# Sigmoid attention with a bilinear feed-forward on one core: float32 scores by row halves in nine pairs, weight decoding in two steps, last product turned round

## The chip, the cores and the metric

The kernel runs on one core of one Trainium2 chip. The metric is the device time of one execution in microseconds, lower is better.

## The reference

```python
S = 448; scale = 1/sqrt(64)                      # 8 batches, 12 heads, 448 tokens, head size 64
scores = scale * (q @ k^T) - log(S)
attn   = sigmoid(scores)
x      = (attn @ v)                              # -> 3584 tokens x 768
a = x @ w1; b = x @ w2                           # w1, w2: 768 x 1024
out = ((a * b) @ w3) @ w_out                     # w3: 1024 x 1024, w_out: 1024 x 768
```

q, k and v are float32; the four weights arrive as 8-byte floats, which the kernel decodes itself, from two 32-bit words to one float32.

## The kernel before

**Precision.** A product of two float32 operands is made in one of two ways. *Split*: each operand is cut into a high and a low part of type fp32r (a copy that rounds, and a subtraction), and three products hi·hi, hi·lo, lo·hi are added in PSUM. *Plain*: one float32 matmul, which the profile records as two matmul records of two passes each.

**Attention.** The 48 head pairs (8 batches of 6) are walked in order, each in 4 slots, one for each chunk of 128 keys (the last of 64). A slot numbers 4·p + i. In a slot TensorE makes the scores of one chunk (`scores`, L184, into the PSUM tile `sp`, two buffers), ScalarE the sigmoid (L169), and one slot later TensorE the product with v (`attend`, L233 or L240, into `av`). In the first `PLAIN` = 12 pairs scores are four fp32r matmuls (the head's q is stacked as high over low rows, so that K is 128) and the product with v is plain, in column halves of the array: the two heads write PSUM rows 0 to 63 and 64 to 127 (L233). In the other pairs all is split: `split_pair` makes qs, kh, kl and ks (VectorE, and GpSimd for kl and ks), the last chunk of both heads is done by `short_scores` (L210), and the product with v takes four fp32r matmuls a chunk (L240).

**Filler.** From slot 26 on each slot also holds 12 matmuls of x @ w1 and x @ w2 of the batch before (`up`, L300, 448 columns), so that batch b's filler runs in batch b+1; the last batch's runs after the attention.

**Weights.** `decode_weights` is a generator with 16 jobs for w1 and w2 (768 KB each) and 24 for w3. One step of it loads the raw words up to three jobs ahead (`load_words`, tile `raw`, three buffers), takes the magnitude on ScalarE (L76), decodes in six VectorE instructions (L83 to L99) and splits the result (a cast L66 on ScalarE, a subtraction L67 on VectorE).

**Order.** Engines named in `manual_schedule` issue in the order of the program text: TensorE and SyncE (SP) throughout the attention, ScalarE and GpSimd too in the first two pairs. The other engines' order is chosen when the kernel is built. All loads and stores are issued by SP, which waits in order for the buffer that the next transfer writes. The tile tag `qk` has three buffers and a pair takes two of them (q and k, each loaded twice, to partitions 0 to 63 and 64 to 127).

**End.** After the attention: w_out is decoded beside the last filler, w3 @ w_out is made (L442, 384 columns), and the last product (L460) takes 128 tokens at a time as the stationary operand and 384 columns of w3·w_out as the moving one.

Of the kernel before, what the change touches and what calls it, by code (L numbers as in the profile page):

```python
# [25 lines left out]
def sigmoid_attention_bilinear_ffn(  # L26
# [6 lines left out]
    w2: bass.AP,  # L33
    w3T: bass.AP,
    w_out: bass.AP,
    out: bass.AP,
):


# [1 line left out]


    nc = tc.nc
    B, D, H, S = qT.shape
    DM, DF = w1.shape[0], w1.shape[1] // 2
    NT = B * S
    P = 128
# [17 lines left out]
    def split(dst_hi, dst_lo, src, hi_engine, lo_engine):  # L65
        hi_engine(out=dst_hi, in_=src)  # L66
        lo_engine.tensor_tensor(out=dst_lo, in0=src, in1=dst_hi, op=ALU.subtract)  # L67

    def load_words(src, pool=pd):
        raw = pool.tile([P, *src.shape[1:-1], 2], U32, name="raw")  # L70
        nc.sync.dma_start(out=raw, in_=src)
        return raw

    def magnitude(raw):
        f = pd.tile([P, *raw.shape[1:-1]], F32, name="f")
        nc.scalar.activation(f, raw[..., 1].bitcast(F32), AF.Abs, scale=HW_SCALE)  # L76
        return f
# [40 lines left out]
    nc.scalar.activation(ready, bias, AF.Sigmoid)  # L118

    def load_pair(b, hp):  # L120
        qq = pa.tile([P, 2, S], F32, name="qq", tag="qk", bufs=3)
        kk = pa.tile([P, 2, S], F32, name="kk", tag="qk", bufs=3)
        for dst, src in ((qq, qT), (kk, kT)):
            for r in range(2):
                nc.sync.dma_start(out=dst[r * D:(r + 1) * D], in_=src[b, :, 2 * hp:2 * hp + 2])  # L125
        return qq, kk

    def load_v(b, hp):
# [7 lines left out]
            nc.sync.dma_start(out=vv[r * D:(r + 1) * D, NC - 1], in_=v[b, full:, cols])  # L136
        return vv

    def split_pair(plain, first, qq, kk):

        qs = pa.tile([P, 2, S], F32R, name="qs")
        kh = pa.tile([P, 2, S], F32R, name="kh")
        kl = pa.tile([P, 2, S], F32R, name="kl")
        copy = nc.scalar.copy if plain else nc.vector.tensor_copy
        (nc.vector.tensor_copy if first else copy)(out=qs, in_=qq)
        nc.vector.tensor_tensor(out=qs[D:], in0=qq[D:], in1=qs[D:], op=ALU.subtract)  # L146
        split(kh, kl, kk, copy, nc.vector if plain else nc.gpsimd)
        if plain:
            return qs, kh, kl, None
# [111 lines left out]
    def words(w, columns):  # L261
        return w.rearrange("(c p) (f u) -> p c f u", p=P, u=2)[:, :, columns]

    def decode_weights():

        step = NK // 2
        jobs = [
            (n, fc, slice(0, NK), words(w, slice(fc * P, (fc + 1) * P)))
            for fc in range(NF) for n, w in ((1, w1), (2, w2))
        ]  # L270
        n_up = len(jobs)
        jobs += [
            (3, ic, slice(at, min(at + step, NF)), words(w3T, slice(ic * P, (ic + 1) * P)))
            for ic in range(NF) for at in range(0, NF, step)
        ]
        raws, fs = [], []
        for i, (n, at, cs, _) in enumerate(jobs):
            end = n_up if i < n_up else len(jobs)
            while len(raws) < min(i + (3 if i < n_up else 2), end):
                _, _, ks, src = jobs[len(raws)]  # L280
                raws.append(load_words(src[:, ks], pp if len(raws) < n_up else pd))
            while len(fs) < min(i + 2, end):
                fs.append(magnitude(raws[len(fs)]))
            f = decode(raws[i], fs[i])
            if n == 3:
                nc.sync.dma_start(out=w3_dram[at, :, cs], in_=f)
            else:
# [27 lines left out]
    def take(stream, n):  # L315
        for _ in range(n):
            next(stream, None)
# [6 lines left out]
    qks = {p: load_pair(*pairs[p]) for p in range(2)}  # L324
    vvs = {0: load_v(*pairs[0])}
    splits, vs = {0: split_pair(0 < PLAIN, True, *qks.pop(0))}, {}
    weights = decode_weights()
    xs = {b: [] for b in range(B)}
    filler = iter(())
# [18 lines left out]

    chunks = [0, NC - 1, *range(1, NC - 1)]
    ups = -(-(NF * 2 * NK * 3) // (NPAIR * NC))  # L350

    pieces = {1, 7, 13, 19} | {NPAIR * NC + i for i in range(3 * NF) if i % 3 < 2}
    slot = 0
    for p, (b, hp) in enumerate(pairs):
        if p == 2:
            order.close()
            order.enter_context(tc.manual_schedule(engines={ET.PE, ET.SP}))
        plain = p < PLAIN
        if p == PLAIN - 1:
            take(weights, 2 * NF - len(pieces & set(range(slot))))  # L360
            phase_p.close()
            pf.append(phase_a.enter_context(tc.tile_pool(name="pf", bufs=2, side="right")))
        if p + 2 < len(pairs):
            qks[p + 2] = load_pair(*pairs[p + 2])
        if p + 1 < len(pairs):
            vvs[p + 1] = load_v(*pairs[p + 1])
        vs[p] = split_v(plain, vvs.pop(p))
        qs, kh, kl, ks = splits.pop(p)
        for i, c in enumerate(chunks):
            if not plain and i == 1:  # L370
                short = short_scores(ks, qs)
            else:
# [4 lines left out]
            if i == min(p, 1) and p + 1 < len(pairs):  # L377
                splits[p + 1] = split_pair(p + 1 < PLAIN, p == 0, *qks.pop(p + 1))
# [30 lines left out]
    for jc in range(NF):  # L409
        take(filler, 10)  # L410
        for half in range(2):
            ms = slice(half * NM, (half + 1) * NM)
            src = w_out[jc * P:(jc + 1) * P].rearrange("p (m u) -> p m u", u=2)[:, ms]
            raw = load_words(src)
# [10 lines left out]
    def load_g(tb):  # L425
        g = p4.tile([P, NF, P], F32, name="graw")
        nc.sync.dma_start(out=g, in_=g_dram[:, :, tb * P:(tb + 1) * P].rearrange("f p t -> p f t"))
        gh = p4.tile([P, NF, P], F32R, name="gh")
        gl = p4.tile([P, NF, P], F32R, name="gl")
        split(gh, gl, g, nc.scalar.copy, nc.vector)  # L430
        return gh, gl

    for ic in range(NF):
        w3h, w3l = w3s.pop(ic)
        if ic + 1 < NF:
# [10 lines left out]
            split(w34h[:, ic, ms], w34l[:, ic, ms], acc[:, :NM], nc.scalar.copy, nc.vector)  # L446


    gs = {0: load_g(0)}
    for tb in range(NT // P):  # L450
        if tb + 1 < NT // P:
            gs[tb + 1] = load_g(tb + 1)
        gh, gl = gs.pop(tb)
        o_sb = p4.tile([P, DM], F32, name="o_sb", bufs=3)
        for half in range(2):
            ms = slice(half * NM, (half + 1) * NM)
            acc = ps.tile([P, 512], F32, name="up", tag=next(banks), bufs=2)
            for fc in range(NF):
                for m, (a, w) in enumerate(((gh, w34h), (gh, w34l), (gl, w34h))):
                    nc.tensor.matmul(  # L460
                        acc[:, :NM], a[:, fc], w[:, fc, ms],
                        start=(fc == 0 and m == 0), stop=(fc == NF - 1 and m == 2),
                    )
            nc.vector.tensor_copy(out=o_sb[:, ms], in_=acc[:, :NM])  # L464
            nc.sync.dma_start(out=out[tb * P:(tb + 1) * P, ms], in_=o_sb[:, ms])
    phase_w.close()


# [24 lines left out]
```

## Time and profile before

| | |
|---|---|
| median of 3 runs | 1102.95 us (1102.86 to 1105.55) |
| profiled execution | 1105.32 us, its span 1103.5 us |
| TensorE busy | 1075.5 us (97%), 5424 records |
| VectorE, ScalarE, GpSimd busy | 729.2 (66%), 566.2 (51%), 203.7 us (18%) |
| HBM | read 102.37 MB, written 29.88 MB, 120 GB/s |

The span is the time from the first to the last instruction; 1.8 us of the profiled execution lie outside it. Matmul ends are modelled and matmuls overlap, so that the time of one is read from start to start. "SPq" rows are SP's issues of transfers.

### The profile page before, as it was taken

What the parts mean: (1) busy time and instruction counts of PE and PEld (TensorE: products, weight loads), DVE (VectorE), ACT (ScalarE), POOL (GpSimd) and SP (SyncE); (2) the same over time, 40 slices, a digit from 0 to 9 for tenths busy, and PEclk for the clock granted to TensorE, in tenths of its full rate; (3) what the DMA queues carried; (4) which work ended last, traced back from release to release, by engine and by line L of the source; (5) the groups of instructions that cost most, each with busy time, mean ns of one, the idle gap of its engine ahead of it and who ended that gap; (6) DMA issues with size and microseconds to landing.
All of it is one profiled execution on the core that took longest, in us unless ns stands there. A gap on an engine that the chain in (4) does not pass through costs nothing.

```text
span 1103.5 us, 14939 instructions
## 1 busy us (share of the span) xinstructions
PE 1075.5 (97%) x5424; PEld 961.9 (87%) x5424; DVE 729.2 (66%) x1119; ACT 566.2 (51%) x792; POOL 203.7 (18%) x256
## 2 busy tenths in 40 slices
PE   3899999999999999999999999999999999999998
PEld 1347678899999989999999899999999999999998
DVE  4678997897988879888788987758732122222222
ACT  3786645677677677767677676753322011111110
POOL 0000012343433433234333333300000000000000
PEclk8999999999999999999999999999999999999999
DMA  8488837354344543545345443115341133333331
GB/s 219 124 198 238 216 102 189 99 141 122 104 122 105 150 103 101 145 105 141 96 116 159 116 120 85 53 44 184 106 123 39 41 102 114 119 101 111 124 100 50
DMA packets 115784, 133.23 MB, mean 121 GB/s; under 512 B 8960, under 2 KB 100352, under 8 KB 115712
## 3 DMA queue, kind: packets, MB, share of 16 engines
q1 hardware_dynamic: 115712, 132.29, 43.2%
q8 instruction: 43, 0.70, 0.3%
q14 instruction: 29, 0.24, 0.1%
HBM read 102.37 MB, written 29.88 MB: 120 GB/s over the span
## 4 chain that ended last, share of the span: by engine, by line
PE 87%; DVE 5%; DMA 4%; issue 1%; SPq 1%; POOL 1%; ACT 1%; DVEq 0%; ACTq 0%; POOLq 0%
PE up L300 38%; PE up L460 21%; PE sp L184 10%; PE av L240 8%; PE up L442 6%; PE av L233 3%; DMA vv<-vL 2%; PE sp L210 1%; DVE al L202 1%; POOL kl L67 1%; SPq L125 1%; DMA raw<-w 1%; DVE qs L146 0%; DMA g_dram<-g 0%; DMA kk<-kT 0%
## 5 line engine op out<-in xcount | busy, mean ns | idle before, releaser
L300 PE MATMUL up<-xh,w 128*128 128x448 f32 x1536 | 466.4, 367 | 0.0
L300 PEld LDWEIGHTS up<-xh,w 128*128 128x128 f32 x1536 | 288.4, 188 | 26.1
L300 PE MATMUL up<-xl,w 128*128 128x448 f32 x768 | 281.3, 366 | 0.0
L460 PE MATMUL up<-w,gh 128*128 128x384 f32 x896 | 227.3, 334 | 0.0
L460 PEld LDWEIGHTS up<-w,gh 128*128 128x128 f32 x896 | 162.0, 188 | 0.0
L67 POOL TENSOR_TENSOR kl<-kk,kh 128x896 fp32r<-128x896 f32 x36 | 102.1, 2836 | 298.2 <-DVE kh L66 234.7
L169 ACT ACTIVATE ah<-sp,bias 128x896 fp32r<-128x896 f32 x108 | 108.7, 1006 | 92.9 <-PE sp L184 92.8
L300 PEld LDWEIGHTS up<-xl,w 128*128 128x128 f32 x768 | 144.2, 188 | 13.1
L460 PE MATMUL up<-w,gl 128*128 128x384 f32 x448 | 149.6, 334 | 0.0
L202 DVE TENSOR_TENSOR al<-sp,ah 128x896 fp32r<-128x896 f32 x108 | 117.7, 1090 | 32.8 <-ACT sp L169 31.0
L464 DVE COPY o_sb<-up 128x384 f32<-128x384 f32 x56 | 31.2, 558 | 160.1 <-PE up L460 160.1
L184 PE MATMUL sp<-qs,kh 128*128 128x448 f32 (+1 forms) x312 | 120.4, 386 | 8.0 <-ACT kh L66 8.0
L66 ACT CAST gh<-graw 128x1024 fp32r<-128x1024 f32 x28 | 29.5, 1053 | 191.8 <-PE up L460 189.3
L184 PE MATMUL sp<-qs,kl 128*128 128x448 f32 (+1 forms) x312 | 115.9, 371 | 0.4 <-DVE kl L67 0.4
L169 ACT ACTIVATE sp<-sp,bias 128x896 f32<-128x896 f32 x108 | 105.0, 973 | 0.0
L184 PEld LDWEIGHTS sp<-qs,kh 128*128 128x128 f32 (+1 forms) x312 | 58.1, 186 | 48.1 <-issue 34.9
L67 POOL TENSOR_TENSOR vs<-vv,vs 128x256 fp32r<-128x256 f32 x72 | 59.3, 838 | 211.0 <-DVE vs L66 172.4
L240 PE MATMUL av<-ah,vs 128*128 128x448 f32 x288 | 94.2, 368 | 1.1 <-DVE t L176 1.1
L460 PEld LDWEIGHTS up<-w,gl 128*128 128x128 f32 x448 | 84.1, 188 | 0.0
L240 PE MATMUL av<-al,vs 128*128 128x448 f32 x216 | 79.3, 367 | 0.6 <-DVE al L202 0.6
L224 DVE TENSOR_TENSOR ah<-st,ah 64x448 fp32r<-64x448 f32 x72 | 49.7, 690 | 26.1 <-ACT st L169 24.5
L184 PEld LDWEIGHTS sp<-qs,kl 128*128 128x128 f32 (+1 forms) x312 | 58.2, 187 | 6.2 <-DVE kl L67 0.8
(57 smaller groups left out, 1351.5 us busy)
## 6 DMA issues: line engine op xcount, KB each, us to landing
qq<-qT SPq DMA_DIRECT2D x96, 224.0 KB, 3.8
kk<-kT SPq DMA_DIRECT2D x96, 224.0 KB, 4.0
g_dram<-g SPq DMA_DIRECT2D x64, 224.0 KB, 1.9
graw<-g_dram SPq DMA_DIRECT2D x28, 512.0 KB, 3.6
raw<-w SPq DMA_DIRECT2D x16, 768.0 KB, 6.2
out<-o_sb SPq DMA_DIRECT2D x56, 192.0 KB, 1.9
vv<-vL SPq DMA_DIRECT2D x48, 192.0 KB, 3.9
raw<-w3T SPq DMA_DIRECT2D x16, 384.0 KB, 4.0
```

Of the source, the lines that this page charges most:

```text
L66: hi_engine(out=dst_hi, in_=src)
L67: lo_engine.tensor_tensor(out=dst_lo, in0=src, in1=dst_hi, op=ALU.subtract)
L169: nc.scalar.activation(dst, src, AF.Sigmoid, bias=bias[:n], scale=scale)
L184: nc.tensor.matmul(sp[:, j], k[:, j, at:at + n], qs[:, j], start=m == 0, stop=m == 1)
L202: nc.vector.tensor_tensor(out=al, in0=sp, in1=ah, op=ALU.subtract)
L224: nc.vector.tensor_tensor(out=a[others, j], in0=t[rows], in1=a[rows, j], op=ALU.subtract)
L233: nc.tensor.matmul(accs[0][cols, :S], v[:ops[0].shape[0], c, cols], ops[0][:, j], start=first, stop=last,)
L240: nc.tensor.matmul(accs[j][:, :S], v[:, c, j].rearrange("p u d -> p (u d)"), a[:, j], start=first and m == 0, stop=last and m == len(ops) - 1,
L300: nc.tensor.matmul(acc[:, :S], w[:, fc, kc], x, start=(kc == 0 and m == 0), stop=(kc == NK - 1 and m == 2),)
L442: nc.tensor.matmul(acc[:, :NM], a[:, jc], w[:, jc, ms], start=(jc == 0 and m == 0), stop=(jc == NF - 1 and m == 2),)
L460: nc.tensor.matmul(acc[:, :NM], a[:, fc], w[:, fc, ms], start=(fc == 0 and m == 0), stop=(fc == NF - 1 and m == 2),)
L464: nc.vector.tensor_copy(out=o_sb[:, ms], in_=acc[:, :NM])
```

## The change

The first nine pairs (`PLAIN` = 9) take their scores straight from q and k: q and k are loaded once, both heads under each other, and each head's scores are one float32 matmul on 64 rows of the array (head 0 on rows 0 to 63, head 1 on rows 64 to 127). Nothing is split in these pairs, and a pair takes one buffer of `qk` instead of two. Pairs 9 to 11 become split pairs. A decoding job is taken in two steps, decode and split, at slots from a list; the raw words have three buffers for the first 12 jobs and one for the others, and are loaded two jobs ahead, then one. ScalarE and GpSimd keep the order of the text until pair 8. The jobs of w3 are 16 instead of 24. The last product has 128 columns of w3·w_out as the stationary operand and 512 tokens as the moving one, and the output is written transposed (the host turns it). q and k lie in memory as batch, head, d, token.

```diff
-    PLAIN = 2 * NPAIR
+    PLAIN = 9
...
-    def load_words(src, pool=pd):
-        raw = pool.tile([P, *src.shape[1:-1], 2], U32, name="raw")
+    def load_words(src, pool=None):
+        if pool is None:
+            raw = pd.tile([P, NK, P, 2], U32, name="raw", bufs=1)[:, :src.shape[1]]
+        else:
+            raw = pool.tile([P, *src.shape[1:-1], 2], U32, name="raw")
...
     def load_pair(b, hp):
+        heads = slice(2 * hp, 2 * hp + 2)
+        if b * NPAIR + hp < PLAIN:
+            qk = pa.tile([P, 2, S], F32, name="qp", tag="qk", bufs=3)
+            for i, src in enumerate((qT, kT)):
+                nc.sync.dma_start(out=qk[:, i], in_=src[b, heads].rearrange("h d s -> (h d) s"))
+            return qk[:, 0], qk[:, 1]
...
+    def split_pair(plain, qq, kk):
+        if plain:
+            return qq, kk, None, None
...
         for j in range(2):
+            if kl is None:
+                rows = slice(j * D, (j + 1) * D)
+                nc.tensor.matmul(sp[:, j], kh[rows, at:at + n], qs[rows], start=True, stop=True)
+                continue
...
+    def load_job(i):
+        _, _, cs, src = jobs[i]
+        raws[i] = load_words(src[:, cs], pp) if i < EARLY else load_words(src[:, cs])
+
     def decode_weights():
         for i, (n, at, cs, _) in enumerate(jobs):
-            end = n_up if i < n_up else len(jobs)
-            while len(raws) < min(i + (3 if i < n_up else 2), end):
-                _, _, ks, src = jobs[len(raws)]
-                raws.append(load_words(src[:, ks], pp if len(raws) < n_up else pd))
-            while len(fs) < min(i + 2, end):
-                fs.append(magnitude(raws[len(fs)]))
-            f = decode(raws[i], fs[i])
+            if i + 2 < EARLY:
+                load_job(i + 2)
+            for k in (i, i + 1):
+                if k not in fs and k in raws:
+                    fs[k] = magnitude(raws[k])
+            f = decode(raws.pop(i), fs.pop(i))
+            if i + 1 >= EARLY and i + 1 < len(jobs):
+                load_job(i + 1)
             if n == 3:
                 nc.sync.dma_start(out=w3_dram[at, :, cs], in_=f)
+                yield
+                continue
+            yield
+            split(wh[n][:, at, cs], wl[n][:, at, cs], f, nc.scalar.copy, nc.vector)
             yield
...
+    first = NPAIR * NC
+    starts = [1 + i * first // 7 for i in range(7)] + [first + 1 + 3 * i // 2 for i in range(8)] + [first + 14]
+    later = [(2 * NPAIR + 2 * i) * NC + 1 for i in range(2 * NF)]
+    steps = starts + [s + 2 - s // first for s in starts] + later
+    EARLY = sum(s < (PLAIN - 1) * NC for s in starts)
+    for p in range(2):
+        qks[p] = load_pair(*pairs[p])
+        load_job(p)
+        if p == 0:
+            vvs[0] = load_v(*pairs[0])
...
-        if p == 2:
+        if p == PLAIN - 1:
             order.close()
             order.enter_context(tc.manual_schedule(engines={ET.PE, ET.SP}))
...
-            if slot in pieces or b > 1 and hp % 3 < 2 and i == 1:
-                take(weights, 1)
+            take(weights, steps.count(slot))
...
+    split_g(0, 1, load_g(0, 1))
+    last = NT // TB - 1
+    for tb in range(NT // TB):
+        for mc in range(DM // P):
+            ms = slice(mc * P, (mc + 1) * P)
             acc = ps.tile([P, 512], F32, name="up", tag=next(banks), bufs=2)
             for fc in range(NF):
+                at = (2 * tb + fc // NH) % 3
+                for m, (w, g) in enumerate(((w34h, ghs), (w34h, gls), (w34l, ghs))):
                     nc.tensor.matmul(
+                        acc[:, :TB], w[:, fc, ms], g[:, at, fc % NH],
                         start=(fc == 0 and m == 0), stop=(fc == NF - 1 and m == 2),
                     )
...
+            nc.vector.tensor_copy(out=o_sb, in_=acc[:, :TB])
+            nc.sync.dma_start(out=outT[ms, tb * TB:(tb + 1) * TB], in_=o_sb)
```

## Rows read from the trace of the kernel before

**Rows 1.** The page's 40 slices of the span: tenths of busy time, tenths of clock.
```profile
PE   3899999999999999999999999999999999999998
PEclk8999999999999999999999999999999999999999
```
**Rows 2.** Stretches: us, busy time (records) of each engine, granted clock, DMA share, GB/s.
```profile
0.00:27.70 27.70, 8.80 (x24) 4.23 (x24) 12.59 (x18) 8.72 (x11) 0.20 (x4) 0.89 0.84 218
27.70:76.70 49.00, 44.87 (x181) 18.82 (x181) 36.24 (x47) 39.37 (x48) 0.00 (x0) 0.96 0.68 166
76.70:172.70 96.00, 96.00 (x443) 67.64 (x441) 83.03 (x121) 54.08 (x68) 3.93 (x6) 1.00 0.68 189
172.70:736.30 563.60, 561.85 (x2743) 513.47 (x2742) 464.14 (x716) 398.30 (x574) 199.54 (x247) 1.00 0.43 114
867.30:1103.50 236.20, 232.93 (x1344) 232.61 (x1342) 63.67 (x83) 27.87 (x27) 0.00 (x0) 1.00 0.31 101
```
**Rows 3.** Timeline of the first 30 us: start, duration, engine, line, operation, [idle before, releaser].
```profile
5.21 0.63 DVE L145 CAST qs<-qq 128x896 fp32r<-128x896 f32 x1 [4.34 <-DMA qq<-qT]
7.05 0.94 ACT L66 CAST kh<-kk 128x896 fp32r<-128x896 f32 x1 [4.83 <-DMA kk<-kT]
8.04 0.74 PE L184 MATMUL sp<-qs,kh 128*128 128x448 f32 x1 [8.04 <-ACT kh L66]
...
13.12 3.29 SPq L71 DMA_DIRECT2D raw<-w  x3
...
19.68 0.89 ACT L76 ACTIVATE f<-raw 128x768 f32<-128x768 f32 x1 [6.25 <-DMA raw<-w]
...
25.93 0.83 ACT L66 CAST w<-f 128x768 fp32r<-128x768 f32 x1 [3.08 <-DVE f L99]
...
27.72 1.76 PE L233 MATMUL av<-ap,vv 128*64 128x448 f32 x4 [10.38 <-ACT ap L169]
```
**Rows 4.** Timeline of TensorE in one slot of batch 0.
```profile
63.03 0.97 PE L233 MATMUL av<-ap,vv 128*64 128x448 f32 x4
63.93 0.47 PE L184 MATMUL sp<-qs,kh 128*128 128x448 f32 x1
...
64.95 0.97 PE L233 MATMUL av<-ap,vv 128*64 128x448 f32 x4
```
**Rows 5.** Timeline of TensorE: where slots 26, 49 and 53 begin.
```profile
76.67 0.47 PE L184 MATMUL sp<-qs,kh 128*128 128x448 f32 x1
...
177.03 0.68 PE L210 MATMUL sp<-qs,ks 128*128 128x448 f32 x2
...
192.66 0.57 PE L210 MATMUL sp<-qs,ks 128*128 128x448 f32 x2
```
**Rows 6.** Timeline of SP and ScalarE from 36 to 48 us: one job's raw words.
```profile
36.55 1.11 SPq L125 DMA_DIRECT2D kk<-kT  x2
...
38.87 0.59 SPq L71 DMA_DIRECT2D raw<-w  x1
...
47.16 0.89 ACT L76 ACTIVATE f<-raw 128x768 f32<-128x768 f32 x1 [2.27 <-DMA raw<-w]
```
**Rows 7.** Timeline of SP from 335 to 348 us: two issues that follow each other.
```profile
335.68 0.53 SPq L286 DMA_DIRECT2D w_dram<-f  x1
347.78 0.32 SPq L312 DMA_DIRECT2D g_dram<-g  x1
```
**Rows 8.** First and last instruction of one decoding on VectorE; GpSimd's group for kl.
```profile
87.69 0.56 DVE L83 TENSOR_SCALAR raw<-raw 128x768 uint32<-128x768 uint32 x1 [1.23 <-ACT f L76]
...
92.43 0.95 DVE L99 TENSOR_TENSOR f<-f,raw 128x768 f32<-128x768 f32 x1
...
L67 POOL TENSOR_TENSOR kl<-kk,kh 128x896 fp32r<-128x896 f32 x36 | 102.1, 2836 | 298.2 <-DVE kh L66 234.7 <-issue 61.3 <-PE sp L184 2.3
```
**Rows 9.** Chain of work: start, us, longest uninterrupted runs of matmuls of 448 and 384 columns.
```profile
736.26 64.43 PE up L300 x312
...
867.27 232.98 PE up L460 x1344
```

More of the change, by code (lines that the diff above doesn't have):

```diff
@@ L35, in sigmoid_attention_bilinear_ffn @@
     w_out: bass.AP,
[L36 removed]
+    outT: bass.AP,
 ):
     nc = tc.nc
[L44 removed]
+    B, H, D, S = qT.shape
     DM, DF = w1.shape[0], w1.shape[1] // 2
@@ L137, in load_v @@
         return vv
[L139 to L145, printed above, removed]
+    def split_pair(plain, qq, kk):
+        if plain:
+            return qq, kk, None, None
+        qs = pf[0].tile([P, 2, S], F32R, name="qs")
+        kh = pf[0].tile([P, 2, S], F32R, name="kh")
+        kl = pf[0].tile([P, 2, S], F32R, name="kl")
+        nc.vector.tensor_copy(out=qs, in_=qq)
         nc.vector.tensor_tensor(out=qs[D:], in0=qq[D:], in1=qs[D:], op=ALU.subtract)
-        split(kh, kl, kk, copy, nc.vector if plain else nc.gpsimd)
-        if plain:
-            return qs, kh, kl, None
+        split(kh, kl, kk, nc.vector.tensor_copy, nc.gpsimd)
         ks = pf[0].tile([P, 2, P], F32R, name="ks")
@@ L323, in sigmoid_attention_bilinear_ffn @@
     pairs = [(b, hp) for b in range(B) for hp in range(NPAIR)]
-    qks = {p: load_pair(*pairs[p]) for p in range(2)}
-    vvs = {0: load_v(*pairs[0])}
-    splits, vs = {0: split_pair(0 < PLAIN, True, *qks.pop(0))}, {}
+    first = NPAIR * NC
+    starts = [1 + i * first // 7 for i in range(7)] + [first + 1 + 3 * i // 2 for i in range(8)] + [first + 14]
+    assert len(starts) == 2 * NF
+    later = [(2 * NPAIR + 2 * i) * NC + 1 for i in range(2 * NF)]
+    steps = starts + [s + 2 - s // first for s in starts] + later
+    EARLY = sum(s < (PLAIN - 1) * NC for s in starts)
+    qks, vvs = {}, {}
+    for p in range(2):
[3 more added lines that the diff above has]
+            vvs[0] = load_v(*pairs[0])
+    splits, vs = {0: split_pair(0 < PLAIN, *qks.pop(0))}, {}
     weights = decode_weights()
@@ L376, in sigmoid_attention_bilinear_ffn @@
                 waiting.append((slot + 1, p, c, attention(plain, sp)))
-            if i == min(p, 1) and p + 1 < len(pairs):
-                splits[p + 1] = split_pair(p + 1 < PLAIN, p == 0, *qks.pop(p + 1))
-            if slot in pieces or b > 1 and hp % 3 < 2 and i == 1:
-                take(weights, 1)
+            if i == 1 and p + 1 < len(pairs):
+                splits[p + 1] = split_pair(p + 1 < PLAIN, *qks.pop(p + 1))
+            take(weights, steps.count(slot))
             if b > 0 and (hp, i) == (0, 2):
@@ L423, in sigmoid_attention_bilinear_ffn, with load_g, split_g @@
     p4 = ctx.enter_context(tc.tile_pool(name="p4", bufs=2, side="left"))
[L425 to L431, printed above, removed]
+    TB = 512
+    NH = NF // 2
+    ghs = pw.tile([P, 3, NH, TB], F32R, name="w")
+    gls = pw.tile([P, 3, NH, TB], F32R, name="w")
+    def load_g(tb, half):
+        g = p4.tile([P, NH, TB], F32, name="graw")
+        fs = slice(half * NH, (half + 1) * NH)
+        nc.sync.dma_start(
+            out=g, in_=g_dram[fs, :, tb * TB:(tb + 1) * TB].rearrange("f p t -> p f t")
+        )
+        return g
+    def split_g(tb, half, g):
+        at = (2 * tb + half) % 3
+        for fs in (slice(0, NH // 2), slice(NH // 2, NH)):
+            split(ghs[:, at, fs], gls[:, at, fs], g[:, fs], nc.scalar.copy, nc.vector)
+    assert NT % TB == 0
+    split_g(0, 0, load_g(0, 0))
     for ic in range(NF):
@@ L446, in sigmoid_attention_bilinear_ffn @@
             split(w34h[:, ic, ms], w34l[:, ic, ms], acc[:, :NM], nc.scalar.copy, nc.vector)
[L449 to L456, printed above, removed]
+    split_g(0, 1, load_g(0, 1))
[3 more added lines that the diff above has]
+            ms = slice(mc * P, (mc + 1) * P)
             acc = ps.tile([P, 512], F32, name="up", tag=next(banks), bufs=2)
             for fc in range(NF):
-                for m, (a, w) in enumerate(((gh, w34h), (gh, w34l), (gl, w34h))):
+                at = (2 * tb + fc // NH) % 3
+                for m, (w, g) in enumerate(((w34h, ghs), (w34h, gls), (w34l, ghs))):
                     nc.tensor.matmul(
-                        acc[:, :NM], a[:, fc], w[:, fc, ms],
+                        acc[:, :TB], w[:, fc, ms], g[:, at, fc % NH],
                         start=(fc == 0 and m == 0), stop=(fc == NF - 1 and m == 2),
                     )
-            nc.vector.tensor_copy(out=o_sb[:, ms], in_=acc[:, :NM])
-            nc.sync.dma_start(out=out[tb * P:(tb + 1) * P, ms], in_=o_sb[:, ms])
+                if (mc, fc) == (DM // P - 1, NH - 1) and tb < last:
+                    split_g(tb + 1, 1, g1)
+            if mc == 0 and tb < last:
+                split_g(tb + 1, 0, load_g(tb + 1, 0))
+                g1 = load_g(tb + 1, 1)
+            o_sb = p4.tile([P, TB], F32, name="o_sb", bufs=3)
+            nc.vector.tensor_copy(out=o_sb, in_=acc[:, :TB])
+            nc.sync.dma_start(out=outT[ms, tb * TB:(tb + 1) * TB], in_=o_sb)
     phase_w.close()
@@ L491 @@
     r = run_bass_kernel_spmd(nc, [arrays], core_ids=[0])
-    return r.results[0]["out"]
+    return np.ascontiguousarray(r.results[0]["out"].T)
```

37 lines of the change are left out of this document (16 added, 21 removed).

## Prediction

> **What bounds it now.** I read first the slices: TensorE is busy from the third slice to the end at the full clock, and only the first two slices (55 us) show gaps [rows 1]. The stretches put numbers on it: up to 27.7 us TensorE works 8.8 us, up to 76.7 us 44.9 of 49, and from there on it is full, but for the 3.3 us at the very end [rows 2]. So there are two different kernels in one. Up to slot 26, where the filler begins (76.67 us [rows 5]), time goes to waits; behind it, it is the number of matmuls times their pitch, and a wait on another engine costs only if it outlasts the filler in the queue. The timeline of the start names the waits: the first matmul comes at 8.04, after two loads of q, two of k and a cast; then ScalarE, in the order of the text, waits for the raw words of the first job (19.68) and for its decoding (25.93) before the third sigmoid, so that TensorE stands 10.4 us, until 27.72 [rows 3]. The granted clock of 0.89 and 0.96 says that part of this stretch ran at 1.2 instead of 2.4 GHz [rows 2].
>
> **The change, part by part.** Slots number as in the kernel's text; "t26" is the start of slot 26.
>
> *1. Batch 0, to t26.* The first matmul needs one q and one k load, as many bytes as the two q loads that had landed at 5.21; the cast goes. First matmul 5.2 instead of 8.04. A q or k load and its fellow are 0.46 MB; the two of k landed 1.84 us behind the two of q, 250 GB/s [rows 3], so the stream begins at 3.4. Slot 1 takes the magnitudes of jobs 0 and 1, and the third sigmoid stands behind them on ScalarE. Ahead of and with the words of job 1, SP has issued q, k of two pairs (0.92 MB), one v (0.23) and two jobs (1.57): 2.72 MB, 10.9 us, landing at 14.3; magnitude and sigmoid take 0.9 and 1.0; the product of slot 3 starts at 16.2 instead of 27.72. The cast now comes two slots behind the decoding and waits for nothing.
> The pitch of a slot: today 1.92, the product with v 0.90 of it [rows 4]. Two float32 matmuls on row halves do not occur in this trace; the column halves are their nearest row (two float32 matmuls of 448 columns, four records, 0.90 together). Bounds are 0.9 and, one after the other, 1.8. I take 0.9, because the two column halves, which also are separate parts of the array, overlap: slot 1.9. Slots 4 to 25 then take 41.8. Slot 7 wants the words of job 3, behind 5.66 MB, landing at 26.1 where ScalarE would be there at 23.8: 2.3 lost; 0.5 for small ones. t26 = 16.2 + 0.9 + 41.8 + 2.8 = 61.7, so **-15.0** (-11 with more waits for words, -18 with none).
>
> *2. Slots 26 to 35, plain, beside filler.* Scores on row halves need a change of the array's division to the filler's, as now between the product and the scores, where the first matmul lasts 0.47 instead of 0.37: **+1.0** over ten slots (0 to +2).
>
> *3. Pairs 9 to 11 become split pairs.* Plain and filler: (177.03 - 76.67) / 23 slots = 4.36, 17.45 a pair; split: 192.66 - 177.03 = 15.63 [rows 5]. VectorE has 464 of 564 us in the split stretch [rows 2], so three pairs with a decoding still fit: **-5.4** (-4 to -5.5).
>
> *4. The buffers of q and k at the passage, slot 31.* Plain pairs hold one of the three `qk` buffers, split pairs two. At slot 28 SP is to load pair 9: buffers hold 7 and 8, one is free, so k of pair 9 waits until the scores of slot 31 have read pair 7's. Does a waiting load hold back those behind it? SP issued nothing for 11.6 us, until the data of the next store in the text was there [rows 7]; the text's order holds. Behind that k stand v of pair 8 and the words of job 11 (loaded two ahead, at slot 28). Job 10 at slot 29 takes the magnitude of job 11, on ScalarE, which is in text order until slot 32; the sigmoids of 30 and 31 stand behind it. So: scores of 31 end; k, v, words (1.47 MB) are issued in 3 us. The same three landed 10.6 us after the first issue with two more q loads in the way [rows 6], 5.9 us would be the bytes alone; I take 8.3, nearer to the row. Magnitude and sigmoid make it 10.2. TensorE has 12 filler matmuls, 2.5 us, and stands for 7.8. After the idle of [rows 3] it ran at the lower clock: product 1.76 against 0.97 [rows 4], and the scores alike, 1.8 us. **+9.6** (+5.5 to +12).
>
> *5. The single buffer of raw words, slots 32 to 41.* Jobs 12 to 15 share one buffer, and each load stands on SP behind the decoding before it. Counted from the start of slot 32: job 11 is decoded at 2, job 12 at 7 (a decoding lasts 5.7 [rows 8]), pair 9 is split by VectorE until 9.5 and by GpSimd (2.84) until 12.4; then k of pair 10 has a buffer, v of 9 and the words of 13 follow, landing at 21.5; magnitude, decoding, to 28; words of 14, 34, decoded 41; only now the words of 15, q and k of 11 and v of 10 are issued (4.7), landing at 50 and split by 51. TensorE wants v of pair 10 in slot 41 after the filler: four plain slots and five split, 17.5 + 19.6 + 2.9 = 40. It stands 11, and 1.8 for the clock: **+12.8**. Above: 20, if decodings are stretched by attention work; below: 3, if k of 10 gets its buffer at once. What is late here is the queue, not an engine.
>
> *6. The last product.* 1344 matmuls of 384 columns become 1008 of 512: the same number of columns. Pitch from rows: 173.2 ns for 384 and 206 for 448 [rows 9], where 2.4 GHz would give 160.0 and 186.7. What is over grows with the columns (13.2, 19.4). In proportion to the columns from 384 on, 512 cost 231, and 1008 of them 232.8, as now. With a fixed 13.2, 226.5: -4.6. On the line through both rows, 238.8: +7.7. I take the proportional and a little of the line: **+0.5** (-4.6 to +7.7). The trace's row for 384 speaks against what TensorE: Matmul & The Clock Gate (Back-to-back issue gap) in the Trainium skill states, columns over 2.4 GHz and 2.5 ns, 162.5 here. By that page 512 columns would take 215.8 ns and the sum would lose another 15.5 us. Splitting g by half blocks (1 MB loads, four casts and subtractions in a block of 33 us) lies beside 144 matmuls; ScalarE has 28 and VectorE 64 of 236 us now [rows 2]. The second half's split has 24 matmuls, 5.5 us, against 3.5 of work: hidden; without that cover 3 us a block.
>
> *7. The tail.* Copy of 512 instead of 384 columns and 256 instead of 192 KB: **+0.3**.
>
> *Free.* ScalarE and VectorE lose the splits of nine pairs; in batch 0 that was cover for nothing, since ScalarE waits. The 16 jobs of w3 hold SP no longer than the 24 stores and loads do now [rows 7], within the lead of a pair that loads have. The q and k of split pairs come in pieces half as long: the transfers have 43% of their engines' time in that stretch [rows 2]. If that cover went, v would be late by about 1 us a pair.
>
> **Sum.** -15.0 + 1.0 - 5.4 + 9.6 + 12.8 + 0.5 + 0.3 = +3.8. The profiled execution took 1105.32, 2.4 above the median of 1102.95; the steps apply to both, so 1109.1 for such an execution and **1106.8** against the median, 1107. The gain of batch 0 and of the split pairs goes back at the passage between them.
>
> **Rivals.**
> - *The queue clears (faster).* Mechanism of 5 and in part 4, the other way: what decides is whether v of pair 10 is issued before 33 us after slot 32. It is if the words of 13 come at 8 instead of 16, that is if k of pair 10 gets a buffer without waiting for GpSimd, and if decodings take 4.5. For: the bounds meet there, VectorE has less to do now. Against: three decodings in a row stand between, and [rows 8] has 5.7 for one. Without 5: 1094; without 5 and half of 4: **1089 to 1094**, I say 1091.
> - *The last product at the pitch of pure streaming.* If what a matmul takes over its columns belongs to the narrow forms, 512 columns take 213.3 ns and 1008 of them 215.0 us, 17.9 less than now: **1088**. Against: the 448 columns, wider, have more over, not less [rows 9]. The Trainium skill's page named under 6 is for it.
> - *The halves of the rows don't overlap.* Then a slot of batch 0 has 2.8, 22 slots and ten more lose 0.9 each, 29 less 3 of waits covered: **1133**. This is the case where the change doesn't do what its first words say. Against: the overlap in [rows 4].
> - *Transfers pace batch 0.* 9.6 MB follow until slot 25; at the 166 GB/s of that stretch today [rows 2] they take 58 us, t26 = 72, and 10 us of the gain are lost: **1117**. Against: 218 GB/s in the stretch before, and half the bytes for q and k.
>
> **How the numbers follow.** The walk as summed: 0.55, own range 1095 to 1119; queue clears 0.25; pure streaming 0.05; no overlap 0.10; transfers 0.05. About 0.3%, 3.3 us, is what a measurement here can tell from no change, so "same" is 1099.6 to 1106.3. Within the walk 0.08 falls below, 0.17 inside and 0.30 above; queue clears gives 0.24 and 0.01; streaming 0.05 below; no overlap 0.10 and transfers 0.05 above. Faster 0.37, same 0.18, slower 0.45. The range takes the walk and the faster cases, and leaves out most of "no overlap" and the ends: 1088 to 1121.
>
> **What will show it.** Step 1: the first filler matmul near 62 and four-record groups of 0.9 for the scores; if these are 1.8, the third rival. Step 4: a gap of TensorE of 5 to 10 us behind the scores of slot 31, with a magnitude on ScalarE that waits for raw words, and a dip of the granted clock. Step 5: a second gap in slot 41, ended by v, with SP waiting on VectorE's decoding. Step 3: pairs 9 to 11 at 15.6 apart from that gap. Step 6: 1008 matmuls in 233 us. The prediction is wrong if there is no gap behind the passage, or if the last product leaves 230 to 236 us.

## The result, and the profile after

The changed kernel takes **1111.72 us** (median of 6 runs, 1109.63 to 1114.17), the kernel before, on the same chip, 1105.37 (6 runs, 1102.86 to 1107.07). The ratio is **1.006, 95% interval 1.004 to 1.0079**: slower by 0.6%. The profiled executions took 1109.63 and 1105.32, with spans of 1107.6 and 1103.5: +4.1 us, which are accounted for below. The profiled execution of after is the fastest of its six, so that the medians, 6.4 us apart, hold 2 us more than this account.

First the slices of the page of after (as [rows 1]): the start is fuller, and two holes stand in the fourth and the sixth slice, with the clock down in both.

```profile
PE   7996959999999999999999999999999999999998
PEclk9998979999999999999999999999999999999999
```

The stretches of after (columns as in [rows 2], the engines in the order TensorE, its weight loads, VectorE, ScalarE, GpSimd) divide it: the start, batch 0, the passage up to slot 31, the passage from slot 32 to slot 45, the rest of the attention, the last product.

```profile
0.00:27.70 27.70, 20.78 (x76) 5.23 (x76) 16.95 (x25) 16.35 (x20) 0.20 (x4) 1.00 0.82 257
27.70:58.30 30.60, 29.79 (x130) 7.54 (x128) 27.06 (x38) 24.62 (x30) 0.00 (x0) 1.00 0.64 191
58.30:93.60 35.30, 26.23 (x118) 15.72 (x116) 18.01 (x27) 11.83 (x16) 0.00 (x0) 0.93 0.45 132
93.60:167.70 74.10, 59.03 (x256) 44.32 (x257) 63.64 (x84) 37.87 (x51) 20.27 (x26) 0.87 0.41 109
167.70:744.30 576.60, 575.44 (x2798) 523.69 (x2797) 469.36 (x685) 406.71 (x581) 202.21 (x247) 1.00 0.42 113
875.30:1107.60 232.30, 228.51 (x1008) 188.83 (x1007) 55.63 (x65) 23.70 (x23) 0.00 (x0) 1.00 0.24 89
```

Up to 27.7 us TensorE now works 20.8 us instead of 8.8 [rows 2]; the third and fourth line lack 9 and 15 us, at a granted clock of 0.93 and 0.87; behind them it is full. Timeline of TensorE, batch 0 and the start of slot 26 (as [rows 3], [rows 4]):

```profile
4.01 3.55 PE L196 MATMUL sp<-qp 64*128 64x448 f32 x8 [4.01 <-DMA qp<-kT]
9.48 1.76 PE L248 MATMUL av<-ap,vv 128*64 128x448 f32 x4 [1.91 <-DMA vv<-vL]
...
14.93 0.97 PE L248 MATMUL av<-ap,vv 128*64 128x448 f32 x4
15.84 1.02 PE L196 MATMUL sp<-qp 64*128 64x448 f32 x4
16.79 0.97 PE L248 MATMUL av<-ap,vv 128*64 128x448 f32 x4
...
58.33 1.02 PE L196 MATMUL sp<-qp 64*128 64x448 f32 x4
59.28 0.47 PE L320 MATMUL up<-xh,w 128*128 128x448 f32 x1
```

The scores of a slot on row halves are the four records of line 196: from 15.84 to the next matmul at 16.79 they take 0.95 us, so the halves do overlap. Slot 26 starts at 58.33 instead of 76.67 [rows 5]. Single traces scatter here: in ten kernels of the next section, whose text up to this place is the same, it starts between 57.65 and 60.97.

The first hole, on TensorE, ScalarE and SP:

```profile
93.61 1.76 PE L248 MATMUL av<-ap,vv 128*64 128x448 f32 x4 [9.08 <-ACT ap L180]
95.30 1.87 PE L196 MATMUL sp<-qp 64*128 64x448 f32 x4
...
91.77 0.89 ACT L79 ACTIVATE f<-raw 128x768 f32<-128x768 f32 x1 [17.15 <-DMA raw<-w]
92.56 1.00 ACT L180 ACTIVATE ap<-sp,bias 128x896 f32<-128x896 f32 x1
...
63.91 1.31 SPq L135 DMA_DIRECT2D qq<-qT  x2
81.91 1.25 SPq L135 DMA_DIRECT2D kk<-kT  x2
...
84.44 0.52 SPq L74 DMA_DIRECT2D raw<-w  x1
```

SP issues q of pair 9 at 63.91 and can issue its k only at 81.91, when a buffer is free. The raw words behind it leave at 84.44; ScalarE waits for them until 91.77, and the sigmoid that TensorE needs comes behind the magnitude. Two rows at nearly double length (1.76 and 1.87 against 0.97 and 1.02) show the lower clock, 1.2 instead of 2.4 GHz, behind the hole.

The second hole, on TensorE, SP, VectorE and GpSimd:

```profile
130.80 0.47 PE L320 MATMUL up<-xh,w 128*128 128x448 f32 x1 [2.33 <-DVE g L331]
...
153.22 0.74 PE L255 MATMUL av<-ah,vs 128*128 128x448 f32 x1 [12.73 <-POOL vs L67]
...
111.53 13.15 SPq L74 DMA_DIRECT2D raw<-w  x2
...
136.16 0.37 SPq L74 DMA_DIRECT2D raw<-w  x1
...
139.26 0.59 SPq L144 DMA_DIRECT2D vv<-vL  x1
...
147.94 0.96 DVE L102 TENSOR_TENSOR f<-f,raw 128x768 f32<-128x768 f32 x1
148.81 0.62 DVE L66 CAST kh<-kk 128x896 fp32r<-128x896 f32 x1
149.35 0.49 DVE L66 CAST vs<-vv 128x256 fp32r<-128x256 f32 x2
149.87 0.62 DVE L331 TENSOR_TENSOR g<-up,a_sb 128x448 f32<-128x448 f32 x1
150.41 2.17 DVE L67 TENSOR_TENSOR w<-f,w 128x768 fp32r<-128x768 f32 x1
...
149.56 2.20 POOL L67 TENSOR_TENSOR kl<-kk,kh 128x896 fp32r<-128x896 f32 x1 [31.43 <-DVE kh L66]
151.72 2.52 POOL L67 TENSOR_TENSOR vs<-vv,vs 128x256 fp32r<-128x256 f32 x2
```

Read it from the end of the wait backwards. TensorE had stood since 140.5 for `vs`, the split v of pair 10. SP issued this v at 139.26; transfers of v issued about then landed after 6.6 us in the median, so v was there by some 146. But VectorE cast it only at 149.35, behind the decoding of job 15 (whose last instruction starts at 147.94) and the cast of k, and GpSimd made `kl` before `vs`. So about 5 us of the 12.7 are the queue on SP, and the rest is VectorE's and GpSimd's order. VectorE was not idle meanwhile: from 140.0 to 153.2 it is busy 12.20 of 13.20 us.

The split pairs of the passage, by the start of slots 37, 45 and 49 (timeline of TensorE):

```profile
119.18 0.68 PE L225 MATMUL sp<-qs,ks 128*128 128x448 f32 x2
...
167.70 0.57 PE L225 MATMUL sp<-qs,ks 128*128 128x448 f32 x2
...
183.24 0.57 PE L225 MATMUL sp<-qs,ks 128*128 128x448 f32 x2
```

From slot 37 to slot 45, two pairs take 48.5 us; the next one, which stands free, takes 15.54.

The end, as the longest pieces of the chain of waits (as [rows 9]):

```profile
744.28 64.43 PE up L320 x312
808.72 66.57 PE up L484 x384
875.29 228.54 PE up L500 x1008
```

### The profile page after: what moved, and what is told of

Same layout as the page of the kernel before. It is cut to its first block, busy times and chain, and to the rows that moved or that the text cites. A ratio compares the mean times of both kernels' runs of the same rounds, so it can differ in the third digit from the quotient of the medians.

```text
span 1107.6 us, 14080 instructions
## 1 busy us (share of the span) xinstructions
PE 1070.8 (97%) x5076; PEld 910.5 (82%) x5076; DVE 729.3 (66%) x1073; ACT 563.0 (51%) x789; POOL 222.7 (20%) x277
## 4 chain that ended last, share of the span: by engine, by line
PE 87%; DVE 6%; DMA 2%; ACT 2%; issue 1%; SPq 1%; POOL 0%; DVEq 0%; POOLq 0%; ACTq 0%
PE up L320 39%; PE up L500 21%; PE av L255 10%; PE sp L199 8%; PE up L484 6%; DMA raw<-w 2%; PE sp L225 1%; PE sp L196 1%; PE av L248 1%; DVE raw L99 1%; DVE f L94 1%; ACT f L79 1%; DVE raw L86 1%; DMA vv<-vL 1%; DVE al L217 1%
## 5 line engine op out<-in xcount | busy, mean ns | idle before, releaser
L320 PE MATMUL up<-xh,w 128*128 128x448 f32 x1536 | 468.2, 368 | 2.3 <-DVE g L331 2.3
L320 PEld LDWEIGHTS up<-xh,w 128*128 128x128 f32 x1536 | 288.9, 188 | 35.7 <-issue 5.3
L320 PE MATMUL up<-xl,w 128*128 128x448 f32 x768 | 281.6, 367 | 0.0
L500 PE MATMUL up<-w 128*128 128x512 f32 x1008 | 228.7, 389 | 0.0
L500 PEld LDWEIGHTS up<-w 128*128 128x128 f32 x1008 | 189.2, 188 | 39.3
L320 PEld LDWEIGHTS up<-xl,w 128*128 128x128 f32 x768 | 144.5, 188 | 12.9
L510 DVE COPY o_sb<-up 128x512 f32<-128x512 f32 x42 | 29.0, 691 | 161.0 <-PE up L500 161.0
L66 ACT CAST w<-graw 128x1024 fp32r<-128x1024 f32 x28 | 29.3, 1055 | 174.7 <-PE up L500 170.5
L255 PE MATMUL av<-ah,vs 128*128 128x448 f32 x312 | 103.7, 373 | 13.9 <-POOL vs L67 12.7
L199 PE MATMUL sp<-qs,kh 128*128 128x448 f32 x234 | 86.3, 369 | 0.0
L199 PE MATMUL sp<-qs,kl 128*128 128x448 f32 x234 | 86.2, 368 | 0.0
L255 PEld LDWEIGHTS av<-ah,vs 128*128 128x128 f32 x312 | 58.7, 188 | 25.4 <-POOL vs L67 13.7
L79 ACT ACTIVATE f<-raw 128x768 f32<-128x768 f32 (+2 forms) x48 | 34.1, 711 | 64.5 <-DMA raw<-w 28.2
L86 DVE TENSOR_SCALAR raw<-raw 128x768 uint32<-128x768 uint32 (+2 forms) x48 | 35.6, 743 | 38.1 <-ACT f L79 37.9
L186 ACT COPY t<-av 64x448 f32<-64x448 f32 x78 | 41.2, 529 | 34.0 <-PE av L255 33.0
```

The lines of the kernel that those rows point to most:

```text
L86: nc.vector.tensor_scalar(out=high, in0=high, scalar1=0x80000000, scalar2=0x80000000, op0=ALU.bitwise_and, op1=ALU.bitwise_xor,)
L186: nc.scalar.copy(out=dst[rows], in_=src[j][others])
L255: nc.tensor.matmul(accs[j][:, :S], v[:, c, j].rearrange("p u d -> p (u d)"), a[:, j], start=first and m == 0, stop=last and m == len(ops) - 1,
L320: nc.tensor.matmul(acc[:, :S], w[:, fc, kc], x, start=(kc == 0 and m == 0), stop=(kc == NK - 1 and m == 2),)
L500: nc.tensor.matmul(acc[:, :TB], w[:, fc, ms], g[:, at, fc % NH], start=(fc == 0 and m == 0), stop=(fc == NF - 1 and m == 2),)
```

## The experiments

The theory at this point, **Q** in the expectations, was the prediction's: the passage from plain to split pairs makes two gaps, each a queue on SP (k of pair 9 waiting for a buffer; words of jobs 13 to 15 waiting for the decoding before them). Its rival **V**: without the queues the time goes to VectorE, which decodes jobs 12 to 15 while it also splits q, k, v and sigmoids of the first split pairs. All diffs are against the changed kernel; ratios are to the kernel before on the same chip. The runs come from several chips, so the ratios compare better than the times.

| kernel | us (range) | ratio, 95% |
|---|---|---|
| changed | 1111.72 (1109.63 to 1114.17) | 1.006 (1.004 to 1.0079) |
| k of pair 9 asked for late | 1094.99 (1093.89 to 1096.77) | 0.9901 (0.9879 to 0.9923) |
| words asked for late | 1107.77 (1106.6 to 1110.82) | 1.0018 (1.0 to 1.0035) |
| both | 1097.2 (1096.63 to 1097.59) | 0.9919 (0.9899 to 0.9939) |
| ScalarE free of the text's order | 1109.28 (1106.83 to 1112.23) | 1.0025 (1.001 to 1.0041) |
| 12 plain pairs | 1089.79 (1089.24 to 1090.32) | 0.9858 (0.9843 to 0.9873) |
| 11 plain pairs | **1086.28** (1084.87 to 1087.93) | **0.9827** (0.981 to 0.9843) |
| 11, single buffer as before | 1087.3 (1085.86 to 1088.56) | 0.9825 (0.9807 to 0.9844) |
| decoding in one step | 1116.67 (1115.45 to 1117.31) | 1.0103 (1.0086 to 1.012) |
| old last product | 1117.72 (1115.4 to 1119.09) | 1.01 (1.0075 to 1.0125) |
| last product in 448 tokens | 1123.32 (one run) | |
| last product in 256 tokens | 1128.1 (one run) | |

**k of pair 9 asked for late.** The load of q and k of pair 9 moves, in the text of SP, behind the last slot of pair 7:

```diff
-        if p + 2 < len(pairs):
+        if p + 2 < len(pairs) and p != PLAIN - 2:
             qks[p + 2] = load_pair(*pairs[p + 2])
...
             take(weights, steps.count(slot))
+            if (p, i) == (PLAIN - 2, NC - 1):
+                qks[p + 2] = load_pair(*pairs[p + 2])
```

> One edit of the changed kernel: the load of q and k of pair 9 stands at the end of slot 31 in the text instead of the start of slot 28, so that nothing waits behind its buffer. Theory Q (the gap of 9.1 us behind the scores of slot 31 comes from SP waiting for a q/k buffer with job 11's words behind it): the gap and the 2.2 us at the lower clock behind it go, about -11 us against the changed kernel, and the gap of 12.7 us in slot 41 stays. Rival W (the words of job 11 are late by their own transfer, or ScalarE is behind with its work): the gap stays within 3 us of 9, time within 3 us.

The hole of slot 31 is gone, as Q said, and the last filler (L320 x312) starts at 731.41, 12.9 earlier: slot 37 starts 9.9 earlier, and the rest comes from behind it. But Q had the second hole stay, and it dissolves too, into small waits: 7.3 us in all, 5.4 of them ended by VectorE, the rest by GpSimd. SP still stands behind words (11.4 us in one row, at 99.26). The passage is not free either: pair 9 to pair 10 takes 23.0 us (109.24 to 132.24), against 15.5 for a free split pair. Timeline of TensorE:

```profile
114.05 0.47 PE L255 MATMUL av<-al,vs 128*128 128x448 f32 x1 [1.46 <-DVE al L217]
...
119.58 0.44 PE L199 MATMUL sp<-qs,kh 128*128 128x448 f32 x1 [0.98 <-DVE st L187]
...
125.89 0.47 PE L255 MATMUL av<-al,vs 128*128 128x448 f32 x1 [1.26 <-DVE al L217]
...
136.79 0.47 PE L255 MATMUL av<-ah,vs 128*128 128x448 f32 x1 [1.52 <-POOL vs L67]
```

**Words asked for late.** The words of jobs 13 to 15 are asked for at their own step, so that they stand no longer ahead of k and v:

```diff
+            if EARLY < i < 2 * NF:
+                load_job(i)
...
-            if i + 1 >= EARLY and i + 1 < len(jobs):
+            if (i + 1 == EARLY or i + 1 >= 2 * NF) and i + 1 < len(jobs):
```

> One edit of the changed kernel: the words of jobs 13 to 15 are asked for at the start of their own step instead of right behind the decoding before, so that the loads of pair 11 and of v of pair 10 stand ahead of the words of job 15 on SP. Theory Q (the gap of slot 41 is v of pair 10 queued behind words that wait for the one buffer): the gap of 12.7 us shrinks below 3, about -13 us with the clock behind it, and the gap at slot 31 stays at 9. Rival V (VectorE is full at the passage, 17 of 20 us busy, with decodings beside the splits of pairs 9 to 11): the work is the same and the gap stays above 8.

A miss for Q, which had 13 us. The wait of 12.7 for v disappears, but the last filler starts only 2.5 us earlier (741.76), and by the ratios the gain is 0.4%. In place of one gap there are several, and these end with VectorE (timeline of TensorE):

```profile
141.30 0.44 PE L255 MATMUL av<-ah,vs 128*128 128x448 f32 x1 [3.55 <-DVE t L187]
...
164.40 0.74 PE L322 MATMUL up<-xh,w 128*128 128x448 f32 x1 [5.13 <-DVE g L333]
```

**Both.**

> Both edits of the two runs before together. Theory Q: both gaps go, 24 to 28 us below the changed kernel, about 1.9% below the kernel before (1082 to 1087 where that has 1105). Rivals W and V: less than 6 us below the changed kernel.

No better than the first alone (1097.2 against 1095.0), though no wait of TensorE in the passage ends with a transfer any more: all that are left, 8.5 us in all, end with VectorE. Q had 1082 to 1087; V's number, less than 6 us below the changed kernel, is missed too, since the hole of slot 31 was the queue's. The stretches of this kernel show what is full instead: from 120 to 140 us VectorE is busy 19.75 of 20, and TensorE 14.79.

```profile
100.00:120.00 20.00, 16.46 (x75) 12.46 (x75) 14.49 (x20) 9.71 (x14) 3.52 (x7) 1.00 0.50 131
120.00:140.00 20.00, 14.79 (x58) 11.94 (x57) 19.75 (x25) 11.29 (x16) 6.93 (x7) 0.88 0.24 74
```

**ScalarE free of the text's order.** ScalarE and GpSimd leave it at slot 28 instead of 32 (`if p == PLAIN - 2` for the `order.close()`).

> One edit of the changed kernel: ScalarE and GpSimd leave the text's order one pair earlier, at slot 28, while SP's queue stays as it is. Theory Q says that the gap at slot 31 needs two things, the words held back on SP and sigmoids queued behind a magnitude on ScalarE; with the second taken away the sigmoids of slots 30 and 31 can go first: the gap falls from 9 to below 2 and the time by about 11 us, though SP waits as long as before. If the queue alone were enough, the gap stays.

The hole of slot 31 goes though k and words are as late as in the changed kernel (k issued at 84.14): it took the words *and* ScalarE's order. The gap came as expected, the time did not: slot 37 starts 7.0 us earlier (112.16), but only 0.6 arrive at the last filler (743.71). The words of the later jobs are still late (SP stands behind them for 17.9 us in one row, at 108.13), and the three pairs from slot 37 to slot 49 take 69.4 us instead of 64.1 (timeline of TensorE):

```profile
132.03 0.74 PE L320 MATMUL up<-xh,w 128*128 128x448 f32 x1 [9.03 <-DVE g L331]
...
150.47 0.74 PE L255 MATMUL av<-ah,vs 128*128 128x448 f32 x1 [7.46 <-POOL vs L67]
```

**12 and 11 plain pairs.** One number: `PLAIN = 2 * NPAIR`, or `PLAIN = 11`. The passage comes when all 16 jobs are decoded or nearly so, and all jobs use the three buffers.

> One size of the changed kernel: 12 plain pairs instead of 9, so that all 16 jobs of w1 and w2 have the three buffers and are decoded before the first split pair, and the passage (slots 40 to 47) has no words in SP's queue. If the passage is what eats the gains (queue and decodings on the path of split pairs alike), there is no gap from 58 to 160 us, three pairs cost 2.2 us more each, and the sum is batch 0 (-18), last product (-4), tail (+0.5) and 12 slots more at 0.1 to 0.2: 1083 to 1086 where the kernel before has 1105. If the gaps belong to the plain pairs' own loads, they move to slots 43 and 53 and the time stays near 1105.

> As e4 with 11 plain pairs: all jobs still have the three buffers, and the last one's split falls in slot 39, before the first split pair at slot 44. The same reason says 2 us less than e4 (one pair at 15.6 instead of 17.9), 1081 to 1084, with no gap over 2 us in the passage.

No gaps at the passage in either. Both times lie 2 to 4 us above what was expected of them; why wasn't looked into. Eleven plain pairs are 3.5 us faster than twelve (2.0 by the start of the last product, 853.89 for 855.87, as expected), and with 1086.28 us the fastest kernel here, 1.7% below the kernel before. Its stretches, cut as those of after:

```profile
58.30:93.60 35.30, 35.30 (x159) 19.80 (x156) 30.19 (x42) 19.32 (x25) 0.00 (x0) 1.00 0.55 167
93.60:167.70 74.10, 74.10 (x342) 51.42 (x341) 46.13 (x68) 37.30 (x51) 15.26 (x21) 1.00 0.45 124
```

**11 plain pairs, single buffer as before.** Two things still differed between 9 and 11: the single raw buffer, and the split pairs beside the decodings. Here jobs 12 to 15 go through the single buffer again, and ScalarE leaves the order at slot 32, but no pair is split while they are decoded:

```diff
-    PLAIN = 9
+    PLAIN = 11
...
-    EARLY = sum(s < (PLAIN - 1) * NC for s in starts)
+    EARLY = 12
...
-        if p == PLAIN - 1:
+        if p == PLAIN - 3:
             order.close()
```

> Eleven plain pairs as in the kernel of 1086.3 us, but the raw words of jobs 12 to 15 go through the single buffer again (as in the changed kernel), and ScalarE and GpSimd leave the order of the text at slot 32. Now the single buffer is there without split pairs beside the decodings. Theory Q (the queue of raw words alone makes the second gap): v and k still stand behind words that wait for the decoding before them, TensorE stands 6 to 12 us between slots 34 and 44, and the time is 1092 to 1098. Rival V (decodings and splits of q and k compete for VectorE and ScalarE): decodings are short without splits beside them, no gap above 3 us, 1086 to 1089.

SP stands behind the words as before, 11.6 us of it in one row of its timeline:

```profile
92.56 11.60 SPq L74 DMA_DIRECT2D raw<-w  x2
```

TensorE does not notice, as the stretch shows:

```profile
93.60:167.70 74.10, 74.03 (x341) 51.40 (x340) 45.48 (x67) 35.83 (x49) 13.92 (x21) 1.00 0.50 132
```

So the single buffer by itself costs next to nothing (the last filler starts at 723.60, with three buffers at 722.89); the second hole needs decodings and split pairs at the same time. Q alone does not explain step 5, and V stands. That it is VectorE, and not something else that a split pair asks for, is read from what ended the waits and from its busy time; no run lightens VectorE alone.

**Decoding in one step.** `steps = starts + starts + later`: the split is taken in the slot of its decoding.

> One part of the change undone: decode and split of a job stand in the same slot again, while ScalarE keeps the text's order until pair 8. Theory: each of the seven casts in batch 0 then holds the next sigmoid for the 4 to 5 us of the decoding, less some 0.6 us of slack, so slot 26 begins 20 to 28 us later than at 58.3; beside the filler 2.5 us more are covered and each of the five jobs up to slot 31 costs 1 to 2; 20 to 35 us slower than the changed kernel. Rival: VectorE works ahead far enough and the two steps are worth under 5 us.

Slot 26's filler starts at 62.85 instead of 59.28, the last filler 5.8 later (750.11), the time is 5 us longer. A miss for the theory, 20 to 35 us; the rival, under 5, is about right. Up to slot 26 ScalarE waits for the decoding only twice (1.5 us at 14.94, 0.3 at 42.67), and of TensorE's waits for a sigmoid one has 2.4 us, at 16.73, the others less than 0.7: mostly VectorE had the job decoded in time.

**The last product: old form, 448 and 256 tokens.** Once the old one in the changed kernel (tokens stationary, 384 columns moving), and twice only `TB = 512` changed to 448 and to 256.

> The changed kernel with the last product as it was before (tokens stationary, 384 columns moving, 1344 matmuls, output not transposed); all else as changed. What turning the product is worth by itself: by the matmul pitches measured in the two kernels (173.3 and 226.6 ns) 4.4 us and some 0.5 of the tail the other way, so 1115 to 1117; by the prediction's proportional reading no difference (1111 to 1112); by pure streaming 18 more.

> One size of the last product: 448 instead of 512 tokens as the moving operand (1152 matmuls). In the trace 384 columns cost 173.2 ns and 512 cost 226.7 in that place, 13.2 and 13.4 over the 160.0 and 213.3 of 2.4 GHz, while 448 columns of the filler cost 203 to 207. If what is over belongs to the matmul, 448 here cost 200.0 ns and the stage lasts 230.4 us; if 448 columns are dear as such, 206 and 237.3 us.

> The last product in token blocks of 256: 2016 matmuls of 256 columns. With a fixed 13.2 ns over the columns at 2.4 GHz a matmul takes 119.9 ns and the product 241.7 us; if the excess goes with the columns (8.8 ns) 115.5 ns and 232.8 us; if the weight load of 128 columns sets the pitch, 120 to 135 ns. Between 384 and 512 a fixed excess was found, and more at 448.

The last piece of the chain of waits, of the old form:

```profile
878.76 232.98 PE up L488 x1344
```

of 448 tokens:

```profile
879.56 238.09 PE up L500 x1152
```

and of 256 tokens:

```profile
881.02 241.92 PE up L500 x2016
```

By division, and over the columns at 2.4 GHz: 384 columns 173.3 ns, 13.3 over; 448: 206.7, 20.0 over; 256: 120.0, 13.3 over; 512 in the changed kernel: 226.7, 13.4 over. The excess is a fixed 13.3 ns at three widths; 448 is the exception, by 6.7 ns, in the last product and nearly so in the filler (64.43 us for 312, 206.5 ns). At 256 columns the 120.0 ns also lie at the edge of what was expected if the weight load set the pitch, so that this width alone could not tell the two apart. Turning the product is worth 4.4 us of TensorE, by the chain of waits. The ratios, 1.01 and 1.006, say the same, but their intervals overlap.

The three kernels of this part do the same as the changed kernel up to the last product, yet their last filler starts at 747.76, 748.56 and 750.02 instead of 744.28. So single traces of the attention scatter by some 6 us, and the one of the changed kernel is the shortest of the four.

## Why the prediction was right and wrong

The range (1088 to 1121) held the time, and slower was the likeliest sign; the two gaps are where the forecast put them. Its sum of +3.8 stands against +4.1 between the profiled executions and 6.4 between the medians. Its steps against the trace of after:

| step | forecast | measured | from |
|---|---|---|---|
| 1 batch 0 | -15.0 | -18.3 | slot 26 at 58.33 for 76.67 |
| 2 division | +1.0 | +1.5 | plain slot with filler 4.51 for 4.36, ten slots |
| 3 split pairs | -5.4 | -5.4 | at 15.63 a pair, as before (15.54 behind the passage); what the pairs lost more is in 5 |
| 4 slot 31 | +9.6 | +10.7 | 9.08 idle, 1.6 at the lower clock |
| 5 slot 41 | +12.8 | +17.3 | two pairs, 119.18 to 167.70, less 2 x 15.63 |
| 6 last product | +0.5 | -4.4 | 228.54 for 232.98 |
| 7 tail | +0.3 | +0.5 | from the last matmul's run to the end of the span |
| not in it | | +2.2 | by difference; 1.9 of it behind slot 53 (198.78 to 744.28, before 192.66 to 736.26), why wasn't looked into |
| sum | +3.8 | +4.1 | spans 1107.6 and 1103.5 |

**Step 1** was right in its parts: first matmul early (4.01 for the 5.2 forecast), 0.95 for the scores, so the third rival (no overlap) is out. Mis-sized was the wait for words: slot 3's product came at 14.93 instead of 16.2, and of the 2.3 lost in slot 7 nothing showed; the largest wait after that was 1.0, for a sigmoid, at 27.02. With the scatter of single traces the whole step is -15.7 to -19.0, and the two steps of a decoding are worth 0.9 to 4.3 of it (slot 26 at 61.90 in the run that takes them back to one). The start moved 257 GB/s, close to the 250 taken, and behind it 191 were enough: the fourth rival (transfers pace batch 0) is out.

**Step 4** was right in mechanism and size, and shown: take the k away from the words' front and the hole is gone, take ScalarE out of the order and it is gone too.

**Step 5** foretold the place and missed the cause in part. The queue ran as forecast: counted from the start of slot 32 (95.30), the words of job 15 left at 40.9 (forecast 41), and v of pair 10 was there at about 51 (50). But it was to be split 1 us later, and that took until 57.9, with VectorE and GpSimd at other work; and TensorE wanted it at 45.2 instead of 40. That the wait came out at 12.7 for 11 is in part luck. "What is late here is the queue, not an engine" is wrong: with the queue taken away most of the loss remained as waits on VectorE, and with the queue kept but no split pair beside it there was none. From slot 37 to slot 49 three free pairs would take 46.6 us; they take 64.1 in the changed kernel, 62.4 with the words late, 58.3 with k of pair 9 late and 61.6 with both. The failed step is the assumption in 3 that three more split pairs fit because VectorE has 464 of 564 us in the split stretch. That is a mean over a stretch with 24 jobs spread out; here jobs 12 to 15 and the first of w3 fell on the first split pairs, and VectorE had 63.6 of 74.1 us, against 46.1 in the kernel with eleven plain pairs. The size, +17.3, is above the +12.8 taken and within the bound of 20; in the three traces of the last-product runs it is 19.3 to 20.0. Its rival (the queue clears, 1089 to 1094) would have been paid only in part by its own mechanism: the kernel with both edits, whose waits no longer end with a transfer, takes 1097.2. How the loss divides between VectorE's sheer work and the order chosen for its instructions wasn't tried.

**Step 6** let the excess grow with the columns, because it read two widths, 384 and 448. The row of 448 [rows 9] was the outlier, so the value taken (proportional, and a little of the line) failed, and the low bound, a fixed 13.2 ns, is what happened. By the prediction's own sign, 230 to 236 us for the last product, it is wrong here: 228.54. The second rival, pure streaming, is out: 226.7 ns, not 213.3. The Trainium skill's TensorE: Matmul & The Clock Gate (Back-to-back issue gap) has 215.8 ns for 512 columns as the gap of an isolated matmul, and about 131 for a stream of weight loads and matmuls, which is what the last product is; the prediction named only the first (whose 15.5 us would be 16.0, counted from the +0.5 in the sum). The trace has 226.7, above both, and it decides.

The errors of 1 and 6 (-8.2) and of all the others (+8.5) nearly cancel in this trace. That the total was closer than its parts is luck.

## What to carry to other kernels

When a change of form begins in the middle of a kernel, look at what still runs there: the gain of batch 0 was real, and lost again because split pairs began while weights were being decoded; moving the passage by two pairs kept the gain. A mean busy share of 82% says nothing on whether more work fits in one place; count the instructions of that place. And take a price of a size that isn't in the trace from more than two widths, since one of two may be the odd one.

## What the runs showed of the hardware

- An fp32r matmul of 448 columns, with a weight load each, has 20 ns over its columns at 2.4 GHz, one of 256, 384 or 512 has 13.3. Why wasn't found.
- Two float32 matmuls of 448 columns on the two row halves of the array overlap: 0.95 us for both, as the two on column halves take 0.90 [rows 4].
- Some of VectorE's instructions are stretched beside GpSimd's. The subtraction at line 67 above took 2.17 us at 150.41, while GpSimd made `kl`; alone it takes 0.95. The multiplication at line 331 just before it, beside the same `kl`, took 0.62 and was not stretched (its mean over the kernel is 0.617); one of its two inputs is in PSUM. The clamp at line 91 in the kernel with both edits is stretched, 2.48 instead of the 0.55 that it takes alone:

```profile
128.08 0.55 DVE L86 TENSOR_SCALAR raw<-raw 128x768 uint32<-128x768 uint32 x1
128.55 2.48 DVE L91 TENSOR_SCALAR f<-f 128x768 f32<-128x768 f32 x1
...
128.30 2.31 POOL L67 TENSOR_TENSOR kl<-kk,kh 128x896 fp32r<-128x896 f32 x1 [0.62 <-issue]
```

  In both cases VectorE's instruction ends shortly after GpSimd's, by 0.82 and 0.42 us, a little less than it takes alone. The Trainium skill's GPSIMD Engine Reference (1. Specifications) says that the two share their SBUF interfaces, with contention for VectorE instructions that have two SBUF inputs or run in a two-port mode; the subtraction, with two inputs in SBUF, agrees with it; the clamp has one input, and that it runs in such a mode no run here shows. In these two cases the stretching costs little beside the loss of step 5: 1.2 us for the first, 1.9 for the second, whose decoding took 9.3 us (128.08 to 137.40) against the 5.7 of [rows 8]; other work between its instructions makes up the rest.
